# Decode attention with a cached key/value stream: picking each partition's own 128 PV columns by four masked VectorE adds before one small product, in place of a ScalarE copy and four small products

## The chip, the cores and the metric

The kernel runs on one core of a Trainium2 chip. The metric is the device time of one execution in microseconds (us); lower is better.

## The reference, cut to what matters

Two identical layers of one-token decoding, for 8 batch rows, 32 heads of 128 columns and 4096 cached keys. Layer 2 reads the same caches again.

```python
def _A_ref(x, k_cache, v_cache, wq, wo):             # x: [8, 1, 640]
    q = (x @ wq).reshape(B, Sq, 32, 128).transpose(0, 2, 1, 3)
    scores = einsum("bhqd,bhkd->bhqk", q, k_cache) * 128 ** -0.5
    o = einsum("bhqk,bhkd->bhqd", softmax(scores), v_cache)
    return o.transpose(0, 2, 1, 3).reshape(B, Sq, 4096) @ wo
def _B_ref(x, w1, w2):                                # 640 -> 1728 -> 640
    return maximum(x @ w1, 0) @ w2
x = x + A(layernorm(x));  x = x + B(layernorm(x))     # and both once more
```

All inputs are bf16. The caches dominate: the core reads 988 MB in an execution.

## The kernel before

The work is cut into 256 *visits*, one for each layer, batch row and pair of heads. A visit loads keys and values into slots of an `arena` in SBUF (26 slots of 512 KB), computes scores, softmax and PV, and frees its slots; a freed slot lets the next load start. A *turn* is the place where the second layer of a batch row begins, with visits of the next row's first layer around it (the prediction calls it the passage from one batch row to the next). There are eight, one for each row. At a turn the feed-forward part, the layer norm and the first queries of the next layer must be ready before its keys can be used, and for some visits the scores are computed with the keys as the stationary operand.

PV is computed on four groups of partitions at once (`c`, at partitions 0, 32, 64 and 96). The stationary operand is four columns of the probabilities, the moving one 4 x 128 columns of values. So row `r` of a group holds four blocks of 128 columns, of which only block `r` is wanted: the sum over keys is a sum of such "diagonal" blocks.

```python
nc.tensor.matmul(                                   # PV, into o_ps
    o_ps[32 * c : 32 * c + CJ, :], lhsT=P_tiles[i][:, h, j : j + CJ],      # CJ = 4
    rhs=arena[:, at + c * CJ * Dh : at + (c + 1) * CJ * Dh], ...)
...
def do_i(i):                                        # row sums of the softmax
    nc.vector.tensor_reduce(out=L, in_=(lsum2_ps if ahead[i] else lsum_ps)..., op=ALU.add)
    nc.vector.reciprocal(out=invL[i], in_=L)

def do_oc(i):                                       # "eviction": PSUM to SBUF
    o_tiles[i] = sm.tile([P, CJ, Dh], BF16, name="o_sb", tag="row", bufs=1)
    nc.scalar.copy(out=o_tiles[i][:OR], in_=o_ps[:OR, :]...)                # OR = 100

def do_og(i):                                       # "the product": sum over keys
    for j in range(CJ):
        nc.tensor.matmul(oy[i][:, :2], lhsT=o_tiles[i][:OR, j, :], rhs=gsel[:OR, j, :],
                         start=(j == 0), stop=(j == CJ - 1))
```

`oy` (columns 0 to 47) and `lsum_ps` (columns 216 to 279) are parts of one 2 KB tile of PSUM, `small_ps`. A planner lays out the order of all work ahead of time; `(6, ("OG", i))` gives it the weight 6 for the product.

## Time and profile before

| | before |
|---|---|
| time, median of 3 runs | 2341.57 us (2341.22 to 2341.63) |
| DMA | 9/10 or more busy in 39 of 40 slices |
| PE / DVE / ACT busy | 60% / 21% / 18% |
| eviction (ACT, 247 times) | 587 ns |
| the product (PE, 4 matmuls a time) | 988 matmuls of 170 ns |

The page of the kernel before: busy time of each engine, GB/s moved in each of 40 slices of the span, and the chain of work that ended last, by engine.

```profile
PE 1398.6 (60%) x18748; PEld 591.4 (25%) x18748; DVE 496.7 (21%) x2022; ACT 426.3 (18%) x986; POOL 59.5 (3%) x296
...
GB/s 411 430 433 401 433 432 432 431 396 432 432 432 430 404 434 431 430 427 403 433 432 431 426 412 434 430 432 420 427 431 427 432 416 430 431 431 431 396 433 329
...
DMA 71%; PE 17%; ACT 6%; DVE 3%; issue 2%; SPq 0%; POOL 0%; ACTq 0%; DVEq 0%; POOLq 0%
```

No compute engine is near its limit: the busiest, PE, is busy 60% of the span. The DMA stream runs at 430 to 434 GB/s in most slices, and every few slices it dips: those are the turns.

Groups of instructions of the kernel before (count | busy us, mean ns of one | idle of the engine just before them, and its main cause):

```profile
L687 PE MATMUL o_ps<-arena,P_sb 128*4 128x512 bf16 x3952 | 584.3, 596 | 402.0 <-DMA arena<-in_A_kv_dram 401.0
...
L795 ACT CAST o_sb<-o_ps 100x512 bf16<-100x512 f32 x247 | 144.9, 587 | 289.3 <-PE o_ps L687 286.0
...
L800 PE MATMUL small_ps<-few,o_sb 100*128 100x2 bf16 x988 | 65.1, 170 | 10.7 <-DVE lsum L787 2.2
```

PE stands 401 us before its PV matmuls, because the values have not arrived: that is slack of PE in the steady stretches. Before the products it stands only 10.7 us in the whole run. The next view is the timeline of the kernel before in a turn (start us, duration us, engine, line, operation, and in brackets the idle time before and its releaser):

```profile
516.26 0.59 ACT L795 CAST o_sb<-o_ps 100x512 bf16<-100x512 f32 x1
...
516.32 0.59 PE L705 MATMUL s_ps<-qo,arena 128*128 128x1 bf16 x16
516.54 0.23 DVE L787 TENSOR_REDUCE lsum<-small_ps 128x2 f32<-128x64 f32 x1 [1.49 <-PE small_ps L781]
...
516.90 0.27 PE L800 MATMUL small_ps<-few,o_sb 100*128 100x2 bf16 x4
```

The copy on ACT takes 0.59 us.

### The profile page before, as it was taken

The numbers are of one execution on the slowest core, as the hardware profiler recorded it, in microseconds if no ns is written. First come the engines' busy times: TensorE is split into PE (matmuls) and PEld (weight loads), VectorE is DVE, ScalarE is ACT, GpSimd is POOL, SyncE is SP. The second block draws the span as 40 slices with busy tenths as digits, with TensorE's granted clock in tenths as the row PEclk, the third lists the DMA queues.
The fourth block names the chain that finished last, engine by engine and source line by source line (L and its number), as shares of the span: only waits on it lengthen the run. The fifth ranks groups of instructions, "written<-read, shape, count | busy, mean of one in ns | idle before, by whom it ended". The sixth has DMA issues, their size and how long they took to land.

```text
span 2343.0 us, 43024 instructions
## 1 busy us (share of the span) xinstructions
PE 1398.6 (60%) x18748; PEld 591.4 (25%) x18748; DVE 496.7 (21%) x2022; ACT 426.3 (18%) x986; POOL 59.5 (3%) x296
## 2 busy tenths in 40 slices
PE   3547654576545764557545675556755567545766
PEld 1214211152111511125111241113411133111523
DVE  1113211131112211122111221112211122111312
ACT  1111211122111221112211121111211112111211
POOL 0000000000000000000000000000000000000000
PEclk9999999999999998555555555555555555555555
DMA  9999999999999999999999999999999999999997
GB/s 411 430 433 401 433 432 432 431 396 432 432 432 430 404 434 431 430 427 403 433 432 431 426 412 434 430 432 420 427 431 427 432 416 430 431 431 431 396 433 329
DMA packets 76753, 990.87 MB, mean 423 GB/s; under 512 B 8596, under 2 KB 8596, under 8 KB 36500
## 3 DMA queue, kind: packets, MB, share of 16 engines
q1 hardware_dynamic: 76564, 988.12, 99.4%
q8 instruction: 146, 2.39, 0.4%
q14 instruction: 43, 0.35, 0.0%
HBM read 988.08 MB, written 0.01 MB: 422 GB/s over the span
## 4 chain that ended last, share of the span: by engine, by line
DMA 71%; PE 17%; ACT 6%; DVE 3%; issue 2%; SPq 0%; POOL 0%; ACTq 0%; DVEq 0%; POOLq 0%
DMA arena<-in_A_kv_dram 71%; PE o_ps L687 5%; PE s_ps L695 4%; PE s_ps L705 2%; ACT P_row L755 2%; ACT o_sb L795 1%; PE small_ps L655 1%; DVE mrow L713 1%; ACT P_sb L761 1%; PE small_ps L800 1%; ACT arena L634 1%; PE small_ps L768 1%; PE small_ps L825 1%; DVE hmx L732 0%; ACT nmax L753 0%
## 5 line engine op out<-in xcount | busy, mean ns | idle before, releaser
L687 PE MATMUL o_ps<-arena,P_sb 128*4 128x512 bf16 x3952 | 584.3, 596 | 402.0 <-DMA arena<-in_A_kv_dram 401.0
L695 PE MATMUL s_ps<-arena,qz 128*4 128x512 bf16 x3040 | 410.3, 602 | 261.1 <-DMA arena<-in_A_kv_dram 249.5
L687 PEld LDWEIGHTS <-P_sb 128*4 128x4 bf16 x3952 | 107.4, 88 | 502.8 <-issue 491.7
L713 DVE TENSOR_REDUCE mrow<-s_ps 100x1 bf16<-100x512 f32 x190 | 131.8, 694 | 323.2 <-PE s_ps L695 323.2
L795 ACT CAST o_sb<-o_ps 100x512 bf16<-100x512 f32 x247 | 144.9, 587 | 289.3 <-PE o_ps L687 286.0
L753 ACT ACTIVATE nmax<-small_ps 100x1 f32<-100x1 f32 x106 | 18.1, 171 | 774.5 <-PE small_ps L742 774.5
L775 DVE CAST P_sb<-small_ps 128x64 bf16<-128x64 f32 x190 | 42.6, 224 | 523.1 <-PE small_ps L768 523.1
L695 PEld LDWEIGHTS <-qz 128*4 128x4 bf16 x3040 | 63.9, 85 | 313.7 <-issue 295.5
L705 PEld LDWEIGHTS <-arena 128*128 128x128 bf16 x4224 | 129.6, 104 | 40.8 <-DMA arena<-in_A_kv_dram 23.4
L705 PE MATMUL s_ps<-qo,arena 128*128 128x1 bf16 x3712 | 123.7, 165 | 17.2 <-ACT P_sb L761 7.6
L768 PE MATMUL small_ps<-few,P_row 100*128 100x16 bf16 x760 | 52.3, 179 | 92.1 <-ACT P_row L755 92.1
L753 ACT ACTIVATE nmax<-small_ps,q_scale 100x1 f32<-100x1 f32 x84 | 22.0, 261 | 398.7 <-PE small_ps L742 398.7
L787 DVE TENSOR_REDUCE lsum<-small_ps 128x2 f32<-128x64 f32 x240 | 53.9, 224 | 171.9 <-PE small_ps L781 171.9
L768 PEld LDWEIGHTS <-P_row 100*128 100x128 bf16 x760 | 35.0, 107 | 186.5 <-ACT P_row L755 178.2
L720 PE MATMUL small_ps<-few,mrow 100*1 100x16 bf16 x190 | 34.4, 181 | 67.6 <-DVE mrow L713 67.6
L755 ACT ACTIVATE P_row<-s_ps,nmax 100x512 bf16<-100x512 f32 x106 | 72.8, 687 | 3.4
L800 PEld LDWEIGHTS <-o_sb 100*128 100x128 bf16 x988 | 45.7, 106 | 107.2 <-ACT o_sb L795 73.8
L655 PE MATMUL small_ps<-xq,wq_sb 128*128 128x1 bf16 x1200 | 48.8, 165 | 38.9 <-DVE qo L812 33.5
L800 PE MATMUL small_ps<-few,o_sb 100*128 100x2 bf16 x988 | 65.1, 170 | 10.7 <-DVE lsum L787 2.2
L727 DVE TENSOR_REDUCE diag<-small_ps 1x2 bf16<-1x16 f32 x190 | 30.8, 162 | 186.9 <-PE small_ps L720 186.9
L720 PEld LDWEIGHTS <-mrow 100*1 100x1 bf16 x190 | 15.0, 79 | 210.8 <-DVE mrow L713 210.8
L755 ACT ACTIVATE P_row<-s_ps,nmax,q_scale 100x512 bf16<-100x512 f32 x84 | 65.3, 778 | 2.8
(225 smaller groups left out, 958.0 us busy)
## 6 DMA issues: line engine op xcount, KB each, us to landing
arena<-in_A_kv_dram SPq DMA_DIRECT2D x124, 4096.0 KB, 23.1
arena<-in_A_kv_dram SPq DMA_DIRECT2D x98, 2048.0 KB, 22.7
arena<-in_A_kv_dram SPq DMA_DIRECT2D x218, 512.0 KB, 6.5
arena<-in_A_kv_dram SPq DMA_DIRECT2D x48, 1024.0 KB, 11.3
arena<-in_A_kv_dram SPq DMA_DIRECT2D x11, 3072.0 KB, 22.4
arena<-in_A_kv_dram SPq DMA_DIRECT2D x11, 2560.0 KB, 20.5
arena<-in_A_kv_dram SPq DMA_DIRECT2D x10, 1536.0 KB, 19.7
wq_sb<-in_A_wq_dram SPq DMA_DIRECT2D x4, 1280.0 KB, 17.6
```

Of the source, the lines that this page charges most:

```text
L655: nc.tensor.matmul(q_ps[:, h : h + 1], lhsT=wq_sb[:, g, c, (2 * n + h) * Dh : (2 * n + h + 1) * Dh], rhs=xlns[b][:, 0, c : c + 1], start=( ...
L687: nc.tensor.matmul(o_ps[32 * c : 32 * c + CJ, :], lhsT=P_tiles[i][:, h, j : j + CJ], rhs=arena[:, at + c * CJ * Dh : at + (c + 1) * CJ * D ...
L695: nc.tensor.matmul(s_ps[32 * c : 32 * c + CJ, :], lhsT=qz[:, i % 3, c // 2, 3 - g : 3 - g + CJ], rhs=arena[:, at + c * BANK : at + (c + 1) ...
L705: nc.tensor.matmul(s_tiles[i][:, j : j + 1], lhsT=arena[:, at + n * P : at + (n + 1) * P], rhs=qo[:, b, h : h + 1], start=True, stop=True,)
L713: nc.vector.tensor_reduce(out=m_tiles[i][:OR, :1], in_=s_ps[:OR], axis=AX.X, op=ALU.max)
L720: nc.tensor.matmul(turn_ps[:1, : 4 * CJ], lhsT=m[:OR, :1], rhs=rsel[:OR], start=True, stop=True)
L755: nc.scalar.activation(out=P_rows[i][:OR], in_=s_ps[:OR], func=ACT.Exp, bias=nm[:OR, :1], scale=more)
L768: nc.tensor.matmul(P_ps[:, k * 4 * CJ : (k + 1) * 4 * CJ], lhsT=P_row[:OR, k * P : (k + 1) * P], rhs=rsel[:OR], start=True, stop=True,)
L775: nc.vector.tensor_copy(out=P_tiles[i].rearrange("p h (c k) -> p h c k", k=BANK // P), in_=P_ps.rearrange("p (k h c) -> p h c k", k=BANK / ...
L787: nc.vector.tensor_reduce(out=L, in_=(lsum2_ps if ahead[i] else lsum_ps).rearrange("p (h j) -> p h j", h=2), axis=AX.X, op=ALU.add)
L795: nc.scalar.copy(out=o_tiles[i][:OR], in_=o_ps[:OR, :].rearrange("p (j d) -> p j d", j=CJ))
L800: nc.tensor.matmul(oy[i][:, :2], lhsT=o_tiles[i][:OR, j, :], rhs=gsel[:OR, j, :], start=(j == 0), stop=(j == CJ - 1))
```

## The change

Its intent: ACT and PE do less. Four masked operations on DVE pick each partition's own block straight from PSUM, so that 256 bytes (128 bf16 columns) remain of each row and one matmul sums over the keys. The diff, cut to its core:

```diff
-                chains.append([(6, ("OG", i)), (0, ("O", i))])
+                chains.append([(2, ("OG", i)), (0, ("O", i))])
...
-    few = consts.tile([P, 2 + 3 * CJ], FP32, name="few")
+    few = consts.tile([P, 3 + 3 * CJ], FP32, name="few")      # + jsel: mask of row r, block r
...
-            P_rows[i] = sm.tile([P, BANK], BF16, name="P_row", tag="row", bufs=1)
+            P_rows[i] = sm.tile([P, BANK], BF16, name="P_row", bufs=1)
...
     def do_oc(i):
-        o_tiles[i] = sm.tile([P, CJ, Dh], BF16, name="o_sb", tag="row", bufs=1)
-        nc.scalar.copy(out=o_tiles[i][:OR], in_=o_ps[:OR, :].rearrange("p (j d) -> p j d", j=CJ))
+        o_tiles[i] = sm.tile([P, Dh], BF16, name="o_sb", bufs=1)
+        o = o_tiles[i][:OR]
+        for j in range(CJ):
+            part, mask = o_ps[:OR, j * Dh : (j + 1) * Dh], jsel[:OR, j : j + 1]
+            if j:
+                nc.vector.scalar_tensor_tensor(out=o, in0=part, scalar=mask, in1=o, op0=ALU.mult, op1=ALU.add)
+            else:
+                nc.vector.tensor_scalar(out=o, in0=part, scalar1=mask, scalar2=None, op0=ALU.mult)
 
     def do_og(i):
-        for j in range(CJ):
-            nc.tensor.matmul(
-                oy[i][:, :2], lhsT=o_tiles[i][:OR, j, :], rhs=gsel[:OR, j, :], start=(j == 0), stop=(j == CJ - 1)
-            )
+        nc.tensor.matmul(oy[i][:, :2], lhsT=o_tiles[i][:OR], rhs=gsel[:OR], start=True, stop=True)
```

Left out: the last 64 rows of `w2` are folded beside each other, so that no half-empty block is loaded, with the matmuls of the feed-forward part to suit. With the new weight the planner groups the loads a little differently: 507 in place of 521.

More of the change, by code (lines that the diff above doesn't have):

```diff
@@ L328 @@
     FC = (Dff + P - 1) // P
-    f_sizes = [min(P, Dff - f * P) for f in range(FC)]
     n_full = Dff // P
@@ L359 @@
     w1_sb = wres.tile([P, DC, Dff], BF16, name="w1_sb")
-    w2_sb = wres.tile([P, FC, D], BF16, name="w2_sb")
+    fold = -(-DC // 2)
+    assert Dff % P == P // 2
+    w2_sb = wres.tile([P, n_full * D + fold * P], BF16, name="w2_sb")
     wq_sb = wres.tile([P, NG, DC, QW], BF16, name="wq_sb")
@@ L374, in load_weights @@
         else:
-            nc.sync.dma_start(out=w2_sb, in_=B_w2.rearrange("p (f n) -> p f n", f=FC))
+            nc.sync.dma_start(out=w2_sb, in_=B_w2)
     load_weights("wq", 0)
@@ L384 @@
     )
-    few = consts.tile([P, 2 + 3 * CJ], FP32, name="few")
-    eps_c, onesb_c, sel = few[:, 0:1], few.bitcast(BF16)[:, 2:3], few.bitcast(BF16)[:, 4:]
+    few = consts.tile([P, 3 + 3 * CJ], FP32, name="few")
+    eps_c, onesb_c, jsel, sel = few[:, 0:1], few.bitcast(BF16)[:, 2:3], few[:, 2 : 2 + CJ], few.bitcast(BF16)[:, 4 + 2 * CJ :]
     nc.vector.memset(eps_c, eps)
@@ L391 @@
     ones_p = _free(onesb_c, [(0, P)])
-    gsel, rsel = sel[:, : 2 * CJ].rearrange("p (j h) -> p j h", h=2), sel[:, 2 * CJ :]
-    nc.vector.memset(sel, 0.0)
+    gsel, rsel = sel[:, :2], sel[:, 2:]
+    nc.vector.memset(few[:, 2:], 0.0)
     for c in range(4):
         rows, at = slice(32 * c, 32 * c + CJ), c // 2 * 2 * CJ + c % 2
-        nc.vector.tensor_copy(out=gsel[rows, :, c // 2], in_=ident[rows, rows])
+        nc.vector.tensor_copy(out=jsel[rows], in_=ident[rows, rows])
+        nc.vector.memset(gsel[rows, c // 2 : c // 2 + 1], 1.0)
         nc.vector.tensor_copy(out=rsel[rows, at : at + 2 * CJ - 1 : 2], in_=ident[rows, rows])
@@ L546, in up @@
             for f in up_parts[k]:
-                fs = f_sizes[f]
-                for c in range(DC):
-                    nc.tensor.matmul(
-                        h[k][:fs, f, :], lhsT=w1_sb[:, c, f * P : f * P + fs], rhs=st["xf"][:, :, c],
-                        start=(c == 0), stop=(c == DC - 1),
-                    )
+                for half in range(1 + (f == n_full)):
+                    rows = slice(half * P // 2, P if f < n_full else half * P // 2 + Dff % P)
+                    for c in range(DC):
+                        nc.tensor.matmul(
+                            h[k][rows, f, :], lhsT=w1_sb[:, c, f * P : min((f + 1) * P, Dff)], rhs=st["xf"][:, :, c],
+                            start=(c == 0), stop=(c == DC - 1), tile_position=(0, rows.start),
+                        )
         def var():
@@ L570, in relu @@
             part = range(FC) if k is None else up_parts[k]
-            for rows, lo, hi in ((P, part[0], min(part[-1] + 1, n_full)), (Dff % P, n_full, part[-1] + 1)):
-                if rows and lo < hi:
-                    nc.vector.tensor_scalar(
-                        out=st["hT"][:rows, lo:hi], in0=h[k or 0][:rows, lo:hi], scalar1=0.0, scalar2=None, op0=ALU.max
-                    )
+            lo, hi = part[0], part[-1] + 1
+            nc.vector.tensor_scalar(out=st["hT"][:, lo:hi], in0=h[k or 0][:, lo:hi], scalar1=0.0, scalar2=None, op0=ALU.max)
         def down(k):
             for c, f in [(k, f) for f in range(FC)] if layer == 0 else [(c, f) for f in up_parts[k] for c in range(DC)]:
-                fs = f_sizes[f]
+                rows = slice(0, P) if f < n_full else slice(c // fold * P // 2, (c // fold + 1) * P // 2)
+                at = f * D + (c % fold if f == n_full else c) * P
                 nc.tensor.matmul(
-                    y[:, c, :], lhsT=w2_sb[:fs, f, c * P : (c + 1) * P], rhs=st["hT"][:fs, f, :],
-                    start=(f == 0), stop=(f == FC - 1),
+                    y[:, c, :], lhsT=w2_sb[rows, at : at + P], rhs=st["hT"][rows, f, :],
+                    start=(f == 0), stop=(f == FC - 1), tile_position=(rows.start, 0),
                 )
@@ L793, in do_oc @@
     def do_oc(i):
-        o_tiles[i] = sm.tile([P, CJ, Dh], BF16, name="o_sb", tag="row", bufs=1)
-        nc.scalar.copy(out=o_tiles[i][:OR], in_=o_ps[:OR, :].rearrange("p (j d) -> p j d", j=CJ))
+        o_tiles[i] = sm.tile([P, Dh], BF16, name="o_sb", bufs=1)
[6 more added lines that the diff above has]
+                nc.vector.tensor_scalar(out=o, in0=part, scalar1=mask, scalar2=None, op0=ALU.mult)
     def do_og(i):
         oy[i] = oy_ps[:, : 2 + DC * B]
-        for j in range(CJ):
-            nc.tensor.matmul(
-                oy[i][:, :2], lhsT=o_tiles[i][:OR, j, :], rhs=gsel[:OR, j, :], start=(j == 0), stop=(j == CJ - 1)
-            )
+        nc.tensor.matmul(oy[i][:, :2], lhsT=o_tiles[i][:OR], rhs=gsel[:OR], start=True, stop=True)
     def do_o(i):
@@ L872, in _laid_out @@
     Dff = B_w1.shape[1]
-    NP, NJ, DC, NG, FC = H // 2, Sk // p, D // p, H // 2 // GP, -(-Dff // p)
+    NP, NJ, DC, NG = H // 2, Sk // p, D // p, H // 2 // GP
     c = np.ascontiguousarray
-    w2 = np.zeros((FC * p, D), B_w2.dtype)
-    w2[:Dff] = B_w2
+    full, fold = Dff // p, -(-DC // 2) * p
+    w2 = np.zeros((p, full * D + fold), B_w2.dtype)
+    w2[:, : full * D] = B_w2[: full * p].reshape(full, p, D).transpose(1, 0, 2).reshape(p, -1)
+    w2[: Dff % p, full * D :] = B_w2[full * p :, :fold]
+    w2[p // 2 : p // 2 + Dff % p, full * D : full * D + D - fold] = B_w2[full * p :, fold:]
     k = A_k_cache.reshape(B, NP, 2, UNIT, Sk // UNIT, Dh).transpose(0, 1, 5, 3, 2, 4).reshape(B, NP, Dh, 2 * Sk)
@@ L889, in _laid_out @@
         "B_w1": c(B_w1.reshape(DC, p, Dff).transpose(1, 0, 2)).reshape(p, -1),
-        "B_w2": c(w2.reshape(FC, p, D).transpose(1, 0, 2)).reshape(p, -1),
+        "B_w2": w2,
     }
```

## The prediction

> **What bounds the kernel now.** The DMA stream. The page shows the DMA engines 9/10 or more busy in 39 of 40 slices, at 430 to 434 GB/s in most, PE busy only 60%, DVE 21%, ACT 18%; the chain of waits is 71% DMA into the arena. 991 MB at 432 GB/s is 2294 us, so 49 us are lost. [...] The losses: the start (366 GB/s in the first 20 us), the last slice (329), and eight dips to 396 to 420 at the turns from one batch row to the next. In 20-us windows there the rate is 368 to 415, with PE busy 15.5 to 17 us. There loads of 512 KB land in 6.5 us instead of 23: little is queued ahead, so a slot freed late is DMA time lost.
>
> **What the change does.**
> - Eviction (247 visits): one ACT copy of 100x512, 587 ns, becomes four dependent DVE operations of 100x128 from PSUM. Estimate: DVE reads of 64 and 512 PSUM columns take 224 and 694 ns, so 128 take 290; a per-partition scalar adds 58 (the 128x5 operation with one takes 223, without 165). So 0.30 to 0.35 us each, 1.3 us together with gaps (1.2 to 1.5): +0.7 us latency. DVE gains some 320 us (21% to 34-35%), ACT loses 145 (18% to 12%).
> - The product: 988 small matmuls and weight loads become 247. The four take 0.27 us to the last result, one 0.17: latency -0.1 us; PE busy falls about 49 us, weight load by 34.
> - w2: 65 KB less, 0.15 us. Up and relu change by under 0.3 us, once at the end.
> - P_row and o_sb stop sharing a buffer; issue order around the turns hardly changes.
> - The planner's weight of the product (6 to 2) regroups loads: 507 instead of 521, more of 4 MB. With packet times from the trace this is about 1.7 us less DMA time.
>
> **On the critical path.** In the steady stretches 8 to 20 us of loads are queued, PE waits for DMA, and nothing of this shows. At a turn PE meets the longer eviction: the small product directly after it waits some 0.7 us longer, and the mean/centre step of the next row, which stands behind the eviction on DVE, is about 1.2 us later. PE waits there for data 1.4 to 3.5 us, which absorbs part. I estimate 0.5 to 1.5 us more DMA idle per turn, plus 0.5 us after the last load. Against it 2 us. Net about +5 us.
>
> **Prediction: 2346.5 us, 8 in 10 between 2338 and 2357.** Faster by over 2%: 0.01; within 2%: 0.97; slower by over 2%: 0.02.
>
> **What would show it.** Right: span within 0.7%; GB/s 430 to 434 in steady slices; HBM bytes 0.07 MB less; DVE about 34%; eviction operations about 0.3 us; waits of PE's small product for DVE o_sb 0.7 us longer than for ACT; the eight dips a little deeper, rates in turn windows 2 to 6% lower. Wrong: dips unchanged or shallower (the turn has more slack than I think, then 2339 to 2341); deeper by over 2 us each (then above 2357).
>
> **What would make it wrong.** DVE operations well above 0.35 us; the stash copies on DVE colliding with the evictions; shifted load groups making or removing a hole.

## The result, and the profile after

| | before | after |
|---|---|---|
| median, us | 2341.58 (2341.22 to 2342.63, 6 runs) | 2366.18 (2363.99 to 2369.2, 6 runs) |
| ratio | | 1.0106 [1.0093, 1.0119] |
| profiled span, us | 2343.0 | 2363.8 |

A ratio here is the mean time of one kernel's fast runs over that of the other's of the same rounds, so it is not quite the ratio of the medians. The changed kernel is plainly slower by 24.6 us (2366.18 − 2341.58), and that lies outside the predicted range. All outputs are right. Kernels are compared only within the same rounds.

The page of the kernel after, the same lines as of the one before:

```profile
PE 1367.4 (58%) x18052; PEld 580.2 (25%) x18052; DVE 819.7 (35%) x3005; ACT 281.1 (12%) x739; POOL 59.0 (2%) x296
...
GB/s 409 430 433 387 413 428 434 430 403 420 434 430 428 385 425 434 431 427 391 435 430 432 424 395 430 432 433 417 413 433 429 433 416 395 433 433 428 392 434 323
...
DMA 65%; PE 20%; DVE 10%; ACT 3%; issue 2%; SPq 0%; DVEq 0%; ACTq 0%
```

The groups of the change:

```profile
L801 DVE SCALAR_TENSOR_TENSOR o_sb<-o_ps,few,o_sb 100x128 bf16<-100x128 f32 x741 | 259.9, 351 | 26.3
...
L803 DVE TENSOR_SCALAR o_sb<-o_ps,few 100x128 bf16<-100x128 f32 x247 | 86.6, 351 | 152.2 <-PE o_ps L688 152.1
...
L807 PE MATMUL small_ps<-few,o_sb 100*128 100x2 bf16 x247 | 42.3, 171 | 166.7 <-DVE lsum L788 159.0
```

The engines' loads moved as intended: ACT has 145 us less, DVE 323 us more, and nobody is near a limit (PE 58% busy, DVE 35%, ACT 12%). The rates of the steady slices are unchanged, still up to 434. But the dips are deeper (the fourth slice 387 after 401, the fourteenth 385 after 404), and the chain now holds 10% DVE in place of 3%. The last line is the key: the product is a quarter of what it was, and PE stands 166.7 us before it, where it stood 10.7.

The timeline of the kernel after, at the same kind of place in a turn:

```profile
237.21 0.35 DVE L803 TENSOR_SCALAR o_sb<-o_ps,few 100x128 bf16<-100x128 f32 x1 [1.22 <-PE o_ps L688]
...
237.27 0.59 PE L706 MATMUL s_ps<-qo,arena 128*128 128x1 bf16 x16
237.60 1.12 DVE L801 SCALAR_TENSOR_TENSOR o_sb<-o_ps,few,o_sb 100x128 bf16<-100x128 f32 x3
238.64 0.21 DVE L788 TENSOR_REDUCE lsum<-small_ps 128x2 f32<-128x64 f32 x1
...
238.91 0.16 PE L807 MATMUL small_ps<-few,o_sb 100*128 100x2 bf16 x1 [1.05 <-DVE lsum L788]
```

The masked operations take 1.47 us together. The row sums, which ran beside the copy, now stand behind them on DVE. The product comes 1.70 us after the eviction's start in place of 0.64. PE has done its 0.59 us of score matmuls and then stands 1.05 us, until the product can run.

The waits of PE over the whole run (us in total, times, longest), first of the kernel before, then of the kernel after, show where else at the turns the same delay appears:

```profile
PE s_ps L695 <- DVE s_ps L671: 6.7, 8, 0.8
...
PE o_ps L680 <- ACT o_sb L795: 3.0, 6, 0.5
...
PE s_ps L492 <- DVE lsum L787: 2.6, 8, 0.4
...
PE small_ps L800 <- DVE lsum L787: 2.2, 5, 0.5
...
PE small_ps L800 <- ACT o_sb L795: 2.1, 9, 0.3
```

```profile
PE small_ps L807 <- DVE lsum L788: 159.0, 147, 1.9
...
PE s_ps L696 <- DVE s_ps L672: 15.8, 8, 2.0
PE s_ps L494 <- DVE lsum L788: 13.7, 8, 1.8
PE o_ps L681 <- DVE o_sb L801: 12.9, 9, 1.5
PE small_ps L807 <- DVE o_sb L801: 7.7, 7, 1.1
```

The lines of L800 and the last line of L807 are waits at the product itself. Beside it, three things that happen once a turn (8 times) each cost PE more: the clearing of `s_ps` on DVE (6.7 to 15.8), the mean of the layer norm (2.6 to 13.7), and PV matmuls that need `o_ps` evicted (3.0 to 12.9). These are 30 us of waiting more, or 3.8 us a turn.

How much of it reaches the DMA? Two sums were worked out from the packet records. The *time lost* is the idle time of the 16 engines plus what each packet took beyond the median of its size, without the start and the end: 23.4 us before, 43.5 after. The *nominal time*, packets times their medians, went from 2317.3 to 2316.0. Together 20.1 − 1.3 = 18.8 us of the 20.8 between the profiled spans; the rest is in the parts left out. (The spans differ by less than the medians because the profiled run of the kernel before took 2344.78 us, 3 us over its median.) Not all of the time lost is idle: counted with 25 us left out at each end, 8 us of the difference are engines less busy and 13 us are packets that took longer than the median of their size. These long packets stand at the turns: there they cost 16.3 us before and 29.4 after, elsewhere 4.0 and 3.6. The lag of the kernel after behind the one before, at the moments when both have moved the same bytes, is a staircase (worked out from the same records):

| us into the run before | 189 | 263 | 471 | 754 | 827 | 1050 | 1124 | 1332 | 1405 | 1613 | 1657 | 1908 | 1980 | 2161 | 2319 |
|---|---|---|---|---|---|---|---|---|---|---|---|---|---|---|---|
| lag, us | 0.4 | 5.2 | 5.0 | 5.7 | 9.8 | 9.3 | 11.1 | 11.0 | 14.0 | 13.9 | 15.8 | 15.3 | 19.6 | 19.6 | 20.2 |

It is flat in the steady stretches and steps up at turns: 20 us over eight turns, 2.5 us each on the mean. The turns are not alike: the second and the last add less than 1 us, the first, third and seventh more than 4.

Around the first such turn the windows show it too (20 us each; busy us of each engine, granted clock, DMA share, GB/s), before and then after:

```profile
200.00:220.00 20.00, 16.09 (x339) 11.51 (x337) 5.31 (x34) 2.77 (x10) 4.53 (x22) 1.00 1.01 383
...
240.00:260.00 20.00, 15.85 (x214) 6.29 (x210) 4.68 (x20) 6.16 (x16) 0.00 (x0) 1.00 1.00 424
```

```profile
200.00:220.00 20.00, 16.00 (x363) 11.74 (x361) 6.88 (x38) 1.59 (x8) 3.22 (x16) 1.00 0.96 346
...
240.00:260.00 20.00, 14.45 (x226) 6.54 (x224) 7.95 (x28) 5.28 (x13) 0.00 (x0) 1.00 0.95 386
```

The rate there is 346 in place of 383 and 386 in place of 424, 9 to 10% less, at the same granted clock of 1.00. Later the clock granted to the kernel after was lower, about 0.5, but that does not make the loss: its six runs had mean clocks from 0.57 (2365.65 us) to 0.741 (2368.73 us), and in `a_both256` below a run at 1.00 took 2398.4 us and one at 0.557 took 2397.59.

### The profile page after: what moved, and what is told of

It is laid out like the page before. It is cut to its first block, busy times and chain, and to the rows that moved or that the text cites. A ratio compares the mean times of both kernels' runs of the same rounds, so it can differ in the third digit from the quotient of the medians.

```text
span 2363.8 us, 42130 instructions
## 1 busy us (share of the span) xinstructions
PE 1367.4 (58%) x18052; PEld 580.2 (25%) x18052; DVE 819.7 (35%) x3005; ACT 281.1 (12%) x739; POOL 59.0 (2%) x296
## 3 DMA queue, kind: packets, MB, share of 16 engines
q8 instruction: 141, 2.31, 0.4%
## 4 chain that ended last, share of the span: by engine, by line
DMA 65%; PE 20%; DVE 10%; ACT 3%; issue 2%; SPq 0%; DVEq 0%; ACTq 0%
DMA arena<-in_A_kv_dram 65%; PE o_ps L688 7%; PE s_ps L696 5%; DVE o_sb L801 4%; PE s_ps L706 3%; ACT P_row L756 1%; DVE o_sb L803 1%; PE small_ps L656 1%; DVE mrow L714 1%; PE small_ps L830 1%; PE small_ps L807 1%; PE small_ps L769 1%; DVE hmx L733 1%; DVE lsum L788 0%; ACT nmax L754 0%
## 5 line engine op out<-in xcount | busy, mean ns | idle before, releaser
L801 DVE SCALAR_TENSOR_TENSOR o_sb<-o_ps,few,o_sb 100x128 bf16<-100x128 f32 x741 | 259.9, 351 | 26.3
L803 DVE TENSOR_SCALAR o_sb<-o_ps,few 100x128 bf16<-100x128 f32 x247 | 86.6, 351 | 152.2 <-PE o_ps L688 152.1
L807 PE MATMUL small_ps<-few,o_sb 100*128 100x2 bf16 x247 | 42.3, 171 | 166.7 <-DVE lsum L788 159.0
L706 PEld LDWEIGHTS <-arena 128*128 128x128 bf16 x4224 | 129.8, 104 | 28.2 <-issue 15.8
L807 PEld LDWEIGHTS <-o_sb 100*128 100x128 bf16 x247 | 25.6, 104 | 243.6 <-DVE o_sb L801 207.4
L817 DVE TENSOR_TENSOR oT<-small_ps,invL 128x2 bf16<-128x2 f32 x120 | 19.1, 159 | 165.5 <-PE small_ps L807 162.9
L656 PE MATMUL small_ps<-xq,wq_sb 128*128 128x1 bf16 x1200 | 48.8, 165 | 33.0 <-DVE qo L817 28.2
```

Of the source, the lines that this page charges most:

```text
L656: nc.tensor.matmul(q_ps[:, h : h + 1], lhsT=wq_sb[:, g, c, (2 * n + h) * Dh : (2 * n + h + 1) * Dh], rhs=xlns[b][:, 0, c : c + 1], start=( ...
L706: nc.tensor.matmul(s_tiles[i][:, j : j + 1], lhsT=arena[:, at + n * P : at + (n + 1) * P], rhs=qo[:, b, h : h + 1], start=True, stop=True,)
L801: nc.vector.scalar_tensor_tensor(out=o, in0=part, scalar=mask, in1=o, op0=ALU.mult, op1=ALU.add)
L803: nc.vector.tensor_scalar(out=o, in0=part, scalar1=mask, scalar2=None, op0=ALU.mult)
L807: nc.tensor.matmul(oy[i][:, :2], lhsT=o_tiles[i][:OR], rhs=gsel[:OR], start=True, stop=True)
```

## The experiments

The theory: at turns hardly any load is queued ahead, so that what PE stands frees slots later and is lost to the DMA, as idle time or as longer packets. In the steady stretches the same standing is free. The records of the kernel before show the difference: at the lowest point of each turn 0.9 to 2.1 us of loads had been issued and not yet landed (their bytes at 434 GB/s), in the steady stretches never less than some 10. In the kernel after the lowest points are 0.2 to 1.4 us. Rivals: the loads that the planner grouped differently; a general cost of the new order in the steady stretches too; and, for the wait itself, its place in PE's queue against the length of the chain to the product.

### 1. The planner's weight alone, both ways

`a_weight6` is the kernel after with the old weight; `b_weight2` the kernel before with the new one.

```diff
-                chains.append([(2, ("OG", i)), (0, ("O", i))])
+                chains.append([(6, ("OG", i)), (0, ("O", i))])
```

> The kernel after, with the planner's weight of the product put back from 2 to 6, so that the loads are grouped as before (521 of them, not 507). Theory latency (each visit near a turn waits about 1 us longer for its eviction, and the DMA queue is empty there): still 18 to 24 us slower than before. Theory plan (the regrouped loads leave the holes): within 6 us of before.

> The kernel before, with only the weight changed from 6 to 2: the loads of after, the eviction of before. Latency: within 4 us of before. Plan: 12 to 22 us slower.

Measured: `a_weight6` 2364.49 us, ratio 1.0102 [1.0087, 1.0118] to the kernel before of the same rounds (2340.81). `b_weight2` 2342.89, ratio 1.0011 [0.9996, 1.0026]. The grouping of loads is not the cause in either kernel.

### 2. The kernel before with a longer eviction

`b_evict2` does ACT's copy twice; nothing of the change is in it.

```diff
-        nc.scalar.copy(out=o_tiles[i][:OR], in_=...)
+        for _ in range(2):
+            nc.scalar.copy(out=o_tiles[i][:OR], in_=...)
```

> The kernel before, with the copy on ACT done twice over (the same result), so that the eviction takes about 0.6 us longer and DVE gets nothing to do. Theory latency: 7 to 17 us slower than before, and the loss at the turns. Theory queue (what costs is DVE work held up behind the masked adds, not the wait of the product): within 4 us of before.

Measured: 2352.89 against 2342.78, ratio 1.0044 [1.0029, 1.0059]: 10.1 us lost by 0.62 us more from eviction to product (1.26 in place of 0.64). So a longer eviction costs time with no work added on DVE. By the same reckoning of the lag, 7.0 of the 7.3 us by which the profiled run fell behind lie within some 90 us around the turns. (Not the product alone came later: PE's waits for `o_sb` before the direct PV matmuls went from 3.0 to 10.1 us too.)

### 3. The old eviction in the turns alone, or in the steady stretches alone

Twelve visits around each turn (88 of the 247 evictions) use ACT's copy and four products again, in `a_turn_copy`; in `a_steady_copy` it is the other 159. The rest of the change stays in both, but for one thing: the row of probabilities `P_row` again shares its buffer with the copy's tile, as in the kernel before.

```diff
+    turn_at = [v for v, (layer, b, hp) in enumerate(visits) if layer and hp == NP - 1]
+    by_copy = [any(t - 4 <= i < t + 8 for t in turn_at) for i in range(len(visits))]   # steady: not any(...)
     def do_oc(i):
+        if by_copy[i]:
+            o_tiles[i] = sm.tile([P, CJ, Dh], BF16, name="o_row", tag="row", bufs=1)
+            nc.scalar.copy(...)                     # and four products in do_og
+            return
```

> The kernel after, but the 12 visits around each turn (4 ahead, 8 from it on; 88 evictions in all) are evicted by one copy on ACT and four products as before; the other 159 keep the four masked adds. Latency at the turns: 2340 to 2345 us, that is 20 us or more of the 24.6 us are back. If the cost lay in the steady stretches (DVE busy 31 to 35 percent there): 2355 or more.

> The mirror image: the 88 evictions around the turns are masked adds, the other 159 one copy on ACT. Latency at the turns: 2361 to 2368 us, nothing or little regained. Cost in the steady stretches: 2350 or less.

Measured: 2358.52 and 2379.34 (ratios 1.0079 and 1.0168). Both missed, and both were slower than expected. The table of selectors had grown by 16 bytes a partition, and the arena behind it had moved in SBUF, in the built program from an offset of 118016 bytes (a multiple of 256) to 118048 (32 beyond one). The same pair was run with padding that put the arena at 118080 (64 beyond one):

> The mix once more, copies at the turns, with the small table of constants padded by 32 bytes so that every later tile, the arena too, starts on a multiple of 64 bytes again, as in before and after (in the first two mixes the arena began 32 bytes past one, and their DMA packets of 32 KB took up to 1224 ns for 1213). Latency at the turns: 2341 to 2347 us. Cost in the steady stretches: 2355 or more.

> The mirror image, padded alike: masked adds in the 88 visits around the turns, the copy in the other 159. Latency at the turns: 2362 to 2369 us. Cost in the steady stretches: 2350 or less.

Measured: 2356.86 and 2375.46 (ratios 1.0062 and 1.0143). Missed again. `a_shift32` measured the shift by itself: the kernel after, with 32 unused bytes.

```diff
-    few = consts.tile([P, 3 + 3 * CJ], FP32, name="few")
+    few = consts.tile([P, 11 + 3 * CJ], FP32, name="few")
```

> The kernel after, with nothing changed but 32 unused bytes in the table of constants, which moves the arena to 32 bytes past a multiple of 64. If the address explains the first mixes: 8 to 14 us slower than after (2373 to 2380), a steady drift, packets of 32 KB at 1213 and 1224 ns. If it was the mixing itself: as after, 2364 to 2369.

Measured: 2382.36, ratio 1.0169 [1.0154, 1.0184] to before: 16 us slower than the kernel after (2366.18; 15 us if each is taken by its ratio to the kernel before of its own rounds), a little over what was expected. The position of the arena matters. By the packet records the commonest durations of a 32 KB packet are 1213 ns with the arena at a multiple of 256 bytes, and 1215 to 1224 ns in these shifted versions. What in the shift makes them longer no run shows.

So the pair was built once more with the arena at 118272, a multiple of 256:

```diff
-    few = consts.tile([P, 3 + 3 * CJ], FP32, name="few")
+    few = consts.tile([P, 64 + 4 * CJ], FP32, name="few")
```

> Copies in the 88 visits around the turns, masked adds in the other 159, the table of constants now widened so that the arena starts on a multiple of 256 bytes, as in before and after. If alignment to 256 bytes was what slowed the first mixes, packets of 32 KB are back at 1213 ns and the time is 2341 to 2347 us under the theory latency at the turns; if the cost lies in the steady stretches, 2355 or more. If the packets stay at 1215 to 1224 ns, the alignment isn't it.

> The mirror image, aligned alike. Latency at the turns: 2362 to 2369 us, as the kernel after. Cost in the steady stretches: 2350 or less.

Measured: `a_turn_copy256` 2343.18 against 2340.99, ratio 1.0009 [0.9995, 1.0023]; `a_steady_copy256` 2364.3, ratio 1.0099 [1.0085, 1.0113]. Both as expected. The whole loss lies in the 88 evictions around the turns. The waits of PE, of `a_turn_copy256` and then of `a_steady_copy256`, say the same thing in the profile:

```profile
PE small_ps L821 <- DVE lsum L790: 99.9, 91, 1.9
...
PE s_ps L698 <- DVE s_ps L674: 6.7, 8, 0.8
...
PE s_ps L496 <- DVE lsum L790: 2.6, 8, 0.4
```

```profile
PE small_ps L821 <- DVE lsum L790: 57.9, 55, 1.2
...
PE s_ps L698 <- DVE s_ps L674: 15.8, 8, 2.0
PE s_ps L496 <- DVE lsum L790: 13.3, 8, 1.9
PE o_ps L683 <- DVE o_sb L809: 12.1, 8, 1.5
PE small_ps L821 <- DVE o_sb L809: 7.7, 7, 1.1
```

In the first PE stands 99.9 us before the product, all of it in the steady stretches, and the time is that of the kernel before. In the second it stands 57.9 us, at the turns, and 23 us are lost. That the wait exists says nothing; where it lies says all. As `a_turn_copy256` keeps the folded `w2` and the new grouping, these together cost about 2 us at most (up to 5 by the interval). The shared buffer of `P_row` is not the cause either: `a_steady_copy256` has it back as well and loses 23 us all the same.

### 4. Both evictions at once

`a_both256` does the copy, the four products *and* the masked adds into a tile that nobody reads. The product's own data come as early as before. Latency alone would cost nothing here. As an edit of `a_turn_copy256`:

```diff
     def do_oc(i):
         if by_copy[i]:                              # True for every visit
             o_tiles[i] = sm.tile([P, CJ, Dh], BF16, name="o_row", tag="row", bufs=1)
             nc.scalar.copy(...)
-            return
-        o_tiles[i] = sm.tile([P, Dh], BF16, name="o_sb", bufs=1)
-        o = o_tiles[i][:OR]
+        o = sm.tile([P, Dh], BF16, name="o_sb", bufs=1)[:OR]   # masked adds as in after
```

> Every visit is evicted by the copy on ACT and four products, and the four masked adds are carried out on DVE as well, into a tile that nobody reads (the result is right). DVE has all the work of after, the product waits for ACT only. Theory latency (the product's wait for the masked adds): within 8 us of before. Theory queue (DVE work behind the masked adds, such as the sum of the exponentials, is what comes late): 15 us or more slower than before.

Measured: 2396.69, ratio 1.0237 [1.0223, 1.0251], 55.7 us slower than before. Its timeline in a turn:

```profile
533.22 0.59 ACT L802 CAST o_row<-o_ps 100x512 bf16<-100x512 f32 x1
...
533.84 0.35 DVE L809 TENSOR_SCALAR o_sb<-o_ps,few 100x128 bf16<-100x128 f32 x1 [1.84 <-ACT o_row L802]
...
535.27 0.21 DVE L790 TENSOR_REDUCE lsum<-small_ps 128x2 f32<-128x64 f32 x1
...
535.53 0.25 PE L815 MATMUL small_ps<-few,o_row 100*128 100x2 bf16 x4 [1.67 <-DVE lsum L790]
```

`o_row` is ready at 533.81, and the product still waits until 535.53, for the row sums behind the masked adds on DVE. Its reason is no datum of the product. Product and row sums touch different columns of one PSUM tile, and the program has a semaphore between them: PE stands 1.67 us and is released by `lsum`. The masked adds wait for ACT's copy in the same way (DVE stands 1.84 us and is released by `o_row`). What would happen without these waits no run shows. So DVE's queue is part of the product's delay, and with the product as late as that (2.31 us) the run could not hold the two theories apart, as it was meant to. Of the 49.7 us by which its profiled run fell behind the one before, 48.5 lie within some 90 us around the turns.

### 5. The copy split between ACT and DVE

`b_split` is the kernel before, with 288 of the 512 columns copied by ACT and the others by DVE.

```diff
-        nc.scalar.copy(out=o_tiles[i][:OR], in_=...)
+        o, cut = o_tiles[i][:OR].rearrange("p j d -> p (j d)"), 288
+        nc.scalar.copy(out=o[:, :cut], in_=o_ps[:OR, :cut])
+        nc.vector.tensor_copy(out=o[:, cut:], in_=o_ps[:OR, cut:])
```

> The kernel before, with the eviction split: ACT copies columns 0 to 287, DVE 288 to 511 at the same time. The eviction should take about 0.4 us instead of 0.59. From the doubled copy (0.6 us more cost 10 us) theory latency expects 1 to 4 us less than before; theory queue expects no gain, or a loss of 1 to 5 us, since the sum of the exponentials now stands behind 0.4 us of DVE work.

Measured: 2344.27, ratio 1.0015 [1.0001, 1.0028]. Its timeline:

```profile
515.82 0.40 ACT L796 CAST o_sb<-o_ps 100x288 bf16<-100x288 f32 x1
...
516.25 0.39 DVE L797 CAST o_sb<-o_ps 100x224 bf16<-100x224 f32 x1 [1.65 <-ACT o_sb L796]
```

The halves did not run side by side: DVE began 0.03 us after ACT had ended. The two engines did not read `o_ps` at the same time (DVE stood 1.65 us and was released by ACT's half), and the split eviction is longer (0.82 us) than the single one (0.59). The loss of 3 us, barely clear of the noise, fits a longer eviction. The shorter one (0.4 us) for which the run was made did not come about.

### 6. The row sums on ACT

In `a_lsum_act` the row sums leave DVE's queue, and the product waits for the masked adds alone.

```diff
-        nc.vector.tensor_reduce(out=L, in_=..., axis=AX.X, op=ALU.add)
+        junk = sm.tile([P, NJ], BF16, name="junk", bufs=1)
+        for h in range(2):
+            nc.scalar.activation(out=junk, in_=...[:, h * NJ : (h + 1) * NJ], func=ACT.Copy, accum_out=L[:, h : h + 1])
```

> The kernel after, with the row sums of the exponentials added up on ACT (two activations with an accumulated output) and not by a reduction on DVE. If the product waits for that reduction because it reads the same PSUM bank, the delay falls from 1.69 to about 1.5 us and the time by 4 to 9 us, to 2357 to 2362. If it waits for the masked adds alone, nothing changes: 2364 to 2369.

Measured: 2366.54, ratio 1.0112: no gain. The delay to the product fell only from 1.69 to 1.57 us, and PE now waits for the masked adds themselves:

```profile
PE small_ps L809 <- DVE o_sb L803: 147.3, 152, 1.7
```

The row sums behind the adds are thus a small part of the delay; the adds are the large one. The DMA time lost was 49.3 us in place of 43.5, but the profiled run was the longest of the four (2371.05). Why not even the 0.12 us showed as time stays open.

### 7. The product later in PE's queue

If standing is the cost, giving PE other work first should win it back. `a_later` puts the product one planner step later; `a_laterq` puts the queries of a later visit one step later as well; `b_laterq` does both to the kernel before.

```diff
-                chains.append([(2, ("OG", i)), (0, ("O", i))])
+                chains.append([(1, None), (2, ("OG", i)), (0, ("O", i))])
```

```diff
-                chains.append(query(visits[i + 2][1], order1.index(visits[i + 2][2])))
+                chains.append([(1, None)] + query(visits[i + 2][1], order1.index(visits[i + 2][2])))
```

> The kernel after, with the product one unit of K matmuls later in PE's order; the query matmuls for a later visit stay in the old place and now come first. If any matmul that writes that bank has to wait for the reduction on DVE, PE stands still at the queries instead: 2359 to 2369. If only the product waits: 2342 to 2352.

> The kernel after, with the product and the queries both one unit later. Theory standing PE: the wait of about 1.05 us at the product shrinks by the 0.5 to 0.6 us of that unit, and the time falls to 2344 to 2354. If the length of the chain from eviction to output itself is what counts, and not PE: 2362 or more.

> The same move in the kernel before, whose product waits little. Theory standing PE: 0 to 3 us faster than before. If the chain's length counts: 2 to 6 us slower.

Measured: `a_later` 2355.39 (1.006 [1.0044, 1.0075]), `a_laterq` 2358.44 (1.0073), `b_laterq` 2341.86 (1.0005 [0.9992, 1.0017]). All three lie between their two expectations, so neither theory is confirmed as it was put. The waits of PE in the turn at 490 to 545 us of `a_later`, with those of the kernel after for the same window behind it:

```profile
PE small_ps L656 <- DVE lsum L788: 3.2, 3, 1.1
PE s_ps L696 <- DVE s_ps L672: 2.0, 1, 2.0
PE s_ps L494 <- DVE lsum L788: 1.7, 1, 1.7
```

```profile
PE small_ps L807 <- DVE lsum L788: 3.2, 3, 1.1
PE s_ps L696 <- DVE s_ps L672: 2.0, 1, 2.0
PE s_ps L494 <- DVE lsum L788: 1.7, 1, 1.7
```

The wait has moved from the product (L807) to the query matmuls that now come first (L656), which also write to `small_ps`, and it is as long as before. Over the whole run some of it is gone: PE waits 90.1 us (L656) and 42.4 us (L807) for `lsum`, where it waited 159.0 in the kernel after, and 11 us of time come back:

```profile
PE small_ps L656 <- DVE lsum L788: 90.1, 85, 1.9
...
PE small_ps L807 <- DVE lsum L788: 42.4, 60, 1.4
```

No order tried removes the wait, and in the kernel before there was nothing to win. No version beats the kernel before.

### The doses together

The delay is from the start of the eviction to the start of the first product matmul, the median over 48 visits at turns, read from the traces. The loss is the difference of medians to the kernel before of the same rounds.

| kernel | delay at turns, us | loss, us |
|---|---|---|
| before | 0.64 | 0 |
| b_split | 1.01 | 3.3 |
| b_evict2 | 1.26 | 10.1 |
| a_lsum_act | 1.57 | 25.2 |
| after | 1.69 | 24.6 |
| a_weight6 | 1.69 | 23.7 |
| a_both256 | 2.31 | 55.7 |
| a_turn_copy256 (1.69 in the steady stretches) | 0.64 | 2.2 |
| a_steady_copy256 (mostly 0.64 in the steady stretches) | 1.69 | 23.3 |

The loss rises with the delay at the turns, and faster than in proportion: the first 0.37 us cost 3 us (barely clear of the noise), the last 0.62 us (from after to `a_both256`) cost 31. That is as it would be if slack absorbed the first part of a delay and little of what goes beyond it; no run took the slack away to test this. Nor is the delay of the product all that differs: what stands behind the eviction on ACT or DVE is later as well. (`a_later`, `a_laterq` and `b_laterq` are left out, as they put other work into the delay.)

## Why the prediction was wrong, point by point

- **"What bounds the kernel: the DMA stream; steady stretches free."** Right. The steady rates are unchanged, and `a_turn_copy256` shows 99.9 us of new waits there that cost nothing.
- **"0.30 to 0.35 us each, 1.3 us together (1.2 to 1.5)."** At the upper edge: 351 ns each, and 1.51 us for the whole eviction on the median. ACT's copy was 0.59. That is 0.92 us more in place of the 0.7 predicted.
- **"DVE gains some 320 us, ACT loses 145."** Right: 323 and 145. **"PE busy falls about 49 us, weight load by 34"** was too high: 31 and 11.
- **"w2: 0.15 us; regrouping 1.7 us less DMA time."** About right: 0.07 MB less is read, and the nominal packet time fell by 1.3 us.
- **"The small product waits some 0.7 us longer."** Mis-sized. The delay grew by 1.05 us (0.64 to 1.69): 0.92 from the eviction, and the row sums come behind it on DVE where they had run beside it, less what the single product saves.
- **"The mean step is about 1.2 us later."** Nearly right: 1.4 us (13.7 − 2.6 over eight). Not seen at all: the clearing of `s_ps` 1.1 us later each turn (15.8 − 6.7), and the direct PV matmuls 1.2 us (12.9 − 3.0).
- **"PE waits there for data 1.4 to 3.5 us, which absorbs part. I estimate 0.5 to 1.5 us more DMA idle per turn."** This is the step that failed. The place and the mechanism were right; the term was too small. As it reads, it counted one product and one mean step a turn. In `a_steady_copy256` the masked adds exist at turns alone, and PE waits there 57.9 + 7.7 us for 62 products (the 7.7, 7 times, are waits for `o_sb` in the same list): about eight a turn, each near 1.06 us. With the mean, the clearing and the PV matmuls that is some 11 us of new waits a turn (an estimate: (65.6 − 4.3 + 10.7 + 9.1 + 9.1) / 8, the first kernel's own waits at its products, 2.2 + 2.1 us in its list above, taken off). Most was absorbed, and 2.5 us a turn was not: 20 us in eight turns, where the prediction had at most 12. Part of the 20 is moreover not idle, which the prediction spoke of, but longer packets.
- **"Deeper by over 2 us each (then above 2357)"** was named as a sign of being wrong, and it is what came. Of the risks named, DVE operations "well above 0.35" did not occur. Stash copies on DVE do come between the product and its reader, but the wait of the queries for that reader did not grow (33.5 us before, 28.2 after). Shifted load groups were cleared by the two runs with the weight exchanged.

Open: how the 2.5 us a turn divide between the product, the mean step and the clearing, which no run separated; why `a_lsum_act` gained nothing; and how much of the 11 us of `a_later` is less standing and how much is another order of work. Also, offsets of 32 and 64 beyond a multiple of 256 bytes were tried, but not 128.

## What to carry to other kernels

When a step moves to another engine, look at what is already queued there and what ran beside the old step: here a 0.59 us copy that cost PE nothing became 1.5 us on the engine that also had to do the row sums, the mean and the clearing. In a DMA-bound kernel do not ask how long the new waits are, but how much is queued ahead where they fall: 100 us of them were free in the steady stretches, and some 90 us at the turns (the estimate above) cost over 20. And count how many times a wait occurs in the tight stretch before allowing for slack: it occurred eight times a turn here, not once.

## What the runs measured of the hardware

- Operations of VectorE and ScalarE on PSUM: with a per-partition scalar, 100x128 took 351 ns on VectorE, both with and without a second tensor operand (`after`, L801 and L803). Without such a scalar 128x64 took 224 ns and 100x512 694 ns (`before`, L775 and L713). On 128x5 operations the scalar cost 58 ns: 223 with (L588), 165 without (L511). The copy of 100x512 on ScalarE took 587 ns (L795).
- Large packets whose destination in SBUF is shifted: a shift of the arena by 32 bytes cost 16 us of 2366 us (`a_shift32`), and the common 32 KB packets went from 1213 ns to as much as 1224 in the shifted versions. A table of constants that grows by some bytes can cause it unseen, as it did by 16 bytes a partition in `a_turn_copy` (2358.52 us; 2343.18 with the arena at a multiple of 256 bytes, `a_turn_copy256`).
- DMA rate: one core loading alone held 430 to 434 GB/s in most of the steady slices here.
- Two engines at one PSUM tile: the row sums on other columns of the tile made the product wait 1.72 us beyond its own data (`a_both256`, 533.81 to 535.53), and a copy split over two engines ran one half after the other (`b_split`, DVE 0.03 us after ACT's end).
- Granted clock: the seven runs of the kernel before that stood beside `a_weight6` had mean granted clocks from 0.557 (2340.81 us) over 0.574 (2337.71 us, the fastest) to 0.763 (2340.87 us): no clear relation to the time of this kernel, which waits for DMA (71% of the chain that ended last).
